# Twelve differences by adding transfers, bfloat16 operands read out of float32 tiles, and a new order of the last steps

## The chip, the core and the metric

The kernel runs on one core of one Trainium2 chip. TensorE (PE in the profile) multiplies matrices; VectorE (DVE) and ScalarE (ACT) work on elements; GpSimd (POOL) and SyncE (SP) here issue work to the 16 DMA engines ("queue" below is the list of transfers that an engine has issued). On-chip data lie in SBUF (128 partitions), results of matmuls in PSUM. The metric is the time of one execution on the device in microseconds; the time before is the median of three runs, 493.36 us (489.19 to 493.4).

## What is computed

Two independent results stand side by side in the output: a Fourier mixing of one input, and a long convolution of the other with kernels made of 128 decaying exponentials for each of 512 channels.

```python
# x: 2048 x 512; dft_seq: 2048 x 2048; dft_hid: 512 x 512
a = einsum("bsd,ed->bse", x, dft_hid_re)
b = einsum("bsd,ed->bse", x, dft_hid_im)
y1 = einsum("ts,bse->bte", dft_seq_re, a) - einsum("ts,bse->bte", dft_seq_im, b)
# u: 2048 x 512; A, C: 512 x 128 (complex); dt: 512
P = exp((A * dt[:, None])[:, :, None] * arange(2048))
K = 2 * einsum("dn,dnl->dl", C, P).real
y2 = irfft(rfft(u.T, 4096) * rfft(K, 4096), 4096)[:, :2048].T + u * D_skip
return concatenate([y1, y2], axis=-1)
```

## The kernel before

The host only rearranges and pads arrays and makes the constant matrices of the short Fourier transforms. One program then does both results at once, and its instructions are ordered by a planner written into the kernel (class `Plan`): each piece of work is a generator that yields the engine it wants and an estimate of its cost, and of all pieces that could start, the one with the earliest start, then the smallest "urgency", is issued next. The order on every queue is therefore fixed when the program is built. `act`, `dve` and `load` give the planner's estimates; `Sem` and `Ring` are counted buffers and `Event` a one-time signal of the planner.

**The Fourier part (`Fnet`).** The matrix along the sequence is loaded as given. Its rows are taken in groups of four that a Fourier matrix would make equal up to sign: for each of four column blocks t, for the sines (c = 1) and cosines (c = 0), and for k = 0 to 3, one load brings a `base` of 128 x 512 float32 and three more blocks of rows into a slot `raw` of 128 x 1536 float32 (`load_quad`, line 392; 32 such groups of rows in all, the `quads`). VectorE forms D, that is `rest` = `raw` plus or minus `base`, in bfloat16 (line 414, and line 419 where single rows have their own sign, k = 0). ScalarE rounds `base` to bfloat16 (`rough`, line 444) and sums the squares of D into a statistic (line 447), from which `guard` decides at the end whether D was small enough; if not, a plain program (`general`) does the Fourier part anew. On TensorE (`sums`, line 497) `base` is multiplied in float32 with the folded input (line 519), D in bfloat16 with the input's differences (line 522) and `rough` in bfloat16 with small parts of the input (`lows`, line 553; `middle`, line 548). `keep` and `keep_low` bring the sums to SBUF, `outputs` multiplies them with the other matrix (lines 611, 612). A base is free again after its four or five matmuls, `rest` too (two buffers), `rough` after its group of sums (six buffers).

**The convolution part (`Ssm`).** The kernels K come from tables of powers. The 512 channels are worked through in 16 chunks of 32. For each chunk ScalarE and VectorE make the seeds (`seed_args`, line 954: arguments by repeated doubling, reduced to half a turn in lines 970 and 972, clamped in line 974, then exponential and sine), and VectorE builds two tables by multiplications and additions (`tables1` and `tables2`, lines 923, 932, 946, 952, 1079). TensorE multiplies the two tables into the taps of the kernel (`taps`, line 1120). For each pair of chunks, 64 channels, `stage1_k` (line 1151) does the first step of the Fourier transform of K, and the result goes through memory (`xk`) to be reloaded in another order. The same is done to u (`stage1_u`, `xu`). The channels form five units of 128, 128, 128, 64 and 64. For each unit and quarter, `product` does the second step (line 1325), the complex product (lines 1355 and 1357; 1343 for the last unit) and the first step back (line 1371); the result `z` goes through memory (`zs`) and is reloaded transposed, and `inverse` does the last step (line 1442) and stores. For the last unit, 4, both trips through memory are replaced by transposes on VectorE (lines 1159 and 1422). The end of the kernel is therefore a chain: the last chunk's tables, its taps, the last `stage1_k` with its transposes, unit 4's product, its transposes, its last step, the store.

The order around the change is set by these lines:

```python
UNITS, LATE, BIGS = ((0, 128), (128, 128), (256, 128), (384, 64), (448, 64)), (3,), 3
FNET, GUARD, XTS = (2.0, 2.0, 2.0, 2.0), 2, 2
ISSUE, LAST_K, LAST_I, LATE_Z = 0.42, 7, 4, 3
BASES, SLOTS, RESTS, STAGED, ROUNDS = 3, 2, 2, 2, 6
GROUP_US, QUAD_US, AHEAD_US = 49.5, 9.0, 20.0
```

`FNET` is the urgency of the Fourier part's matmuls. A group's load isn't issued before GROUP_US x (its number // 4) + QUAD_US x (its number % 4) - AHEAD_US on the planner's clock. `LATE` names the unit whose product on VectorE waits until all tables are done.

Of the kernel before, what the change touches and what calls it, by code (L numbers as in the profile page):

```python
# [57 lines left out]
ARGS = 0.3  # L58
# [134 lines left out]
def load(kb):  # L193
    return max(0.55, kb / 330)


class Fnet:
# [11 lines left out]
    def __init__(self, tc, ctx, plan, x, wT, sT, out):  # L209
# [6 lines left out]
        self.ys, self.rounds = Sem(STAGED), Sem(ROUNDS)  # L216
# [153 lines left out]
    def loads(self, b):  # L370
# [3 lines left out]
        for n, i in enumerate(self.quads):  # L374
# [15 lines left out]
            self.plan.spawn(self.load_quad(i, slots), urgency)  # L390

    def load_quad(self, i, raw):
# [3 lines left out]
        first = i == self.quads[0]  # L396
# [13 lines left out]
        yield self.rests  # L410
        rest = self.pool.tile([128, 3, DM], BF16, name="rest", bufs=RESTS)

        def same(lo, hi, step, n, op):
            return v.tensor_tensor(rest[:, lo:hi:step], raw[:, lo:hi:step],  # L414
                                   base[:, None, :].to_broadcast([128, n, DM]), op=op)

        def own(lo, hi, sign):
            n = hi - lo
            return v.scalar_tensor_tensor(rest[:, lo:hi].rearrange("p n t -> p (n t)") if n == 1 else rest[:, lo:hi],
                                          base if n == 1 else base[:, None, :].to_broadcast([128, n, DM]),  # L420
                                          self.sign[:, sign:sign + 1],
                                          raw[:, lo:hi].rearrange("p n t -> p (n t)") if n == 1 else raw[:, lo:hi],
                                          op0=OP.mult, op1=OP.add)
        steps = {
            (0, 0): [(1536, lambda: same(0, 3, 1, 3, OP.subtract))],
            (0, 1): [(512, lambda: same(0, 1, 1, 1, OP.subtract)), (1024, lambda: same(1, 3, 1, 2, OP.add))],
            (1, 0): [(1024, lambda: same(0, 2, 1, 2, OP.add)), (512, lambda: same(2, 3, 1, 1, OP.subtract))],
            (1, 1): [(1024, lambda: same(0, 3, 2, 2, OP.add)), (512, lambda: same(1, 2, 1, 1, OP.subtract))],
        }[t // 2, c]
        if not k and (t, c) == (1, 0):  # L430
# [1119 lines left out]
```

## Time and profile before

| what | value |
|---|---|
| median of three runs | 493.36 us (489.19, 493.4, 493.36) |
| the profiled execution | 494.64 us |
| its span in the profile | 492.8 us |
| granted TensorE clock in it, mean | 0.932 of full speed |
| moved by the transfers | 110.42 MB, 224 GB/s over the span |

The span runs from the first to the last recorded instruction; the rest of the execution's time lies around it. In the profile a group of instructions is given as line, engine, operation, output<-inputs, shapes and count, then the busy time in us and the mean of one in ns, then the idle time of the engine just before them with what ended it. A float32 matmul shows as two records, its two passes. Matmuls are pipelined, so that their records overlap and a busy TensorE is not one at its peak; VectorE's records overlap a little too.

### The profile page before, as it was taken

How to read it: one execution, taken by the hardware profiler on the slowest of the kernel's cores; microseconds unless marked ns; L12 is line 12 of the kernel's file. 1: busy time of each engine (PE TensorE's matmuls, PEld its weight loads, DVE VectorE, ACT ScalarE, POOL GpSimd, SP SyncE). 2: the span in 40 equal slices, each digit the busy share in tenths (PEclk: the TensorE clock that was granted, in tenths of full speed). 3: DMA queues.
4: the chain of work that ended last, by engine and by line, in shares of the span. 5: the costliest groups of instructions: out<-in, count | busy, mean ns of one | idle time of the engine just before them, and what ended most of it. 6: DMA issues, size and time to landing. Idle time of an engine off the chain costs nothing. (4 is left out here: it accounts for less than half of the span.)

```text
span 492.8 us, 13631 instructions
## 1 busy us (share of the span) xinstructions
PE 396.8 (81%) x5630; PEld 200.9 (41%) x5674; DVE 440.8 (89%) x774; ACT 362.6 (74%) x725; POOL 0.9 (0%) x14
## 2 busy tenths in 40 slices
PE   3659977999869659989689877999997589788853
PEld 3213314344424425435253424454455254445642
DVE  3999997999999999999999999899999999996342
ACT  1658999999999697867597997879888896351420
POOL 0000000000000000000000000000000000000000
PEclk9977988999979897999899989999999799899995
DMA  8996794986558993878964299177678937965642
GB/s 292 359 352 200 275 354 171 306 289 238 156 194 261 283 281 98 274 196 283 343 202 165 50 285 319 46 209 244 205 247 228 253 94 224 227 179 211 177 132 63
DMA packets 130546, 110.42 MB, mean 224 GB/s; under 512 B 57136, under 2 KB 101552, under 8 KB 129968
## 3 DMA queue, kind: packets, MB, share of 16 engines
q1 hardware_dynamic: 122512, 106.48, 69.5%
q10 hardware_dynamic: 7968, 3.02, 2.2%
q8 instruction: 46, 0.75, 0.6%
q14 instruction: 20, 0.16, 0.1%
HBM read 77.04 MB, written 32.44 MB: 222 GB/s over the span
## 5 line engine op out<-in xcount | busy, mean ns | idle before, releaser
L923 DVE TENSOR_TENSOR prod<-t,cs 128x1024 f32<-128x1024 f32 (+4 forms) x160 | 125.1, 798 | 5.0 <-ACT t L1038 3.5
L611 PE MATMUL f<-p,w 128*128 128x512 f32 x128 | 70.2, 630 | 7.8 <-ACT y L636 5.7
L932 DVE TENSOR_TENSOR t<-prod 128x512 f32<-128x512 f32 (+4 forms) x160 | 73.6, 477 | 0.6
L447 ACT ACTIVATE slots<-rest 128x1536 f32<-128x1536 bf16 x32 | 47.4, 1481 | 14.6 <-DVE rest L414 13.5
L414 DVE TENSOR_TENSOR rest<-slots,base 128x512 bf16<-128x512 f32 (+2 forms) x52 | 53.6, 1034 | 0.7 <-PE f L522 0.5
L519 PE MATMUL f<-base,es 128*128 128x512 f32 x64 | 39.8, 708 | 13.7 <-ACT bes L332 6.6
L1120 PE MATMUL f<-t,t 128*32 128x80 f32 x2048 | 42.0, 238 | 10.7 <-DVE t L932 5.7
L1120 PEld LDWEIGHTS f<-t,t 128*32 128x32 f32 x2048 | 37.6, 112 | 20.3 <-issue 10.3
L939 ACT ACTIVATE square<-t 128x256 f32<-128x256 f32 (+1 forms) x64 | 36.6, 571 | 12.1 <-DVE t L932 6.8
L1079 DVE TENSOR_TENSOR t<-t,cs 128x1024 f32<-128x1024 f32 x32 | 39.0, 1220 | 0.0
L519 PE MATMUL f<-base,ec 128*128 128x512 f32 x64 | 36.5, 653 | 0.0
L611 PEld LDWEIGHTS f<-p,w 128*128 128x128 f32 x128 | 22.3, 193 | 32.0 <-issue 16.8
L522 PE MATMUL f<-rest,xi 128*128 128x512 bf16 x88 | 28.4, 422 | 7.9 <-DVE rest L414 5.5
L522 PE MATMUL f<-rest,xr 128*128 128x512 bf16 x88 | 26.3, 397 | 7.5 <-DVE rest L414 6.0
L1325 PE MATMUL f<-big,w 64*32 64x256 f32 (+1 forms) x960 | 27.4, 358 | 4.7 <-issue 3.3
L1350 ACT ACTIVATE big<-f 128x1024 f32<-128x1024 f32 x26 | 25.8, 1026 | 4.3 <-PE f L1325 4.3
L952 DVE TENSOR_TENSOR t<-square 128x128 f32<-128x128 f32 (+1 forms) x64 | 24.8, 387 | 1.2 <-ACT square L939 1.1
L522 PEld LDWEIGHTS <-xi 128*128 128x128 bf16 x96 | 9.8, 104 | 36.6 <-issue 28.2
L798 ACT ACTIVATE mid<-f 128x512 f32<-128x512 f32 x24 | 13.2, 591 | 14.0 <-PE f L1371 14.0
L1325 PEld LDWEIGHTS f<-big,w 64*32 64x32 f32 x960 | 16.0, 108 | 17.3 <-issue 8.4
L946 DVE SCALAR_TENSOR_TENSOR t<-t 128x128 f32<-128x128 f32 (+2 forms) x48 | 22.4, 466 | 0.4
L522 PEld LDWEIGHTS <-xr 128*128 128x128 bf16 x96 | 9.7, 101 | 31.6 <-issue 28.1
(174 smaller groups left out, 720.7 us busy)
## 6 DMA issues: line engine op xcount, KB each, us to landing
slots<-in_sT SPq DMA_DIRECT2D x31, 768.0 KB, 5.6
xu<-big SPq DMA_DIRECT2D x16, 512.0 KB, 4.1
base<-in_sT SPq DMA_DIRECT2D x31, 256.0 KB, 4.8
big<-xu SPq DMA_DIRECT2D x13, 512.0 KB, 7.3
big<-xk SPq DMA_DIRECT2D x13, 512.0 KB, 6.9
xk<-big SPq DMA_DIRECT2D x6, 1024.0 KB, 7.0
zs<-mid SPq DMA_DIRECT2D x11, 512.0 KB, 4.5
big<-zs SPq DMA_DIRECT2D x10, 512.0 KB, 7.9
```

Of the source, the lines that this page charges most:

```text
L414: return v.tensor_tensor(rest[:, lo:hi:step], raw[:, lo:hi:step], base[:, None, :].to_broadcast([128, n, DM]), op=op)
L447: nc.scalar.activation(raw, rest, AF.Square, accum_out=self.stat[:, n:n + 1])
L519: nc.tensor.matmul(out, x[:, cols], base, start=k == 0, stop=False)
L522: nc.tensor.matmul(out, still[:, cols], rest[:, h], start=False, stop=k == 3 and h == 2)
L611: nc.tensor.matmul(ps, self.w[k][:, cols], self.p[t, c][:, d], start=k == 0, stop=False)
L923: self.nc.vector.tensor_tensor(p.rearrange("p k d c m -> p k (d c) m"), src.rearrange("p d c l -> p (d c) l")[:, None, :, rows].to_broadca ...
L932: self.nc.vector.tensor_tensor(dst[:, :, :, rows], p[:, 0], p[:, 1, :, ::-1], op=OP.add)
L939: self.nc.scalar.activation(sq, t[:, :, :, m // 2:m], AF.Square)
L1079: self.nc.vector.tensor_tensor(t[:, :, ::1 - 2 * k, 48 + 16 * k:64 + 16 * k], t[:, :, :, 1:32:2], cs[:, k, 5, :, :, None].to_broadcast([12 ...
L1120: nc.tensor.matmul(ps[32 * j:32 * j + 32, i], t1[:, d, c], t2[:, d, c], start=c == 0, stop=c == 1, tile_position=(0, 32 * j))
L1325: nc.tensor.matmul(both[:, :, c], self.w2[rows, R * q + r, xx, 32 * c:32 * c + 32], xs[rows, r, xx], start=True, stop=True, tile_position= ...
L1350: a.activation(flat[:, 1024 * m:1024 * m + 1024], p.rearrange("p b d -> p (b d)"), AF.Copy)
```

## The change

- **D.** For twelve groups of rows (`ADDED`: the sines of each t, k = 1, 2, 3) D is no longer made by VectorE. `base` is loaded once more into those blocks of `raw` to which it is to be added (one transfer with a repeated source), ScalarE writes -`base` into the block from which it is to be subtracted, and a transfer issued by GpSimd adds the rows from memory onto `raw`. For the other twenty groups VectorE makes D in place, in float32.
- **Upper halves.** There is no `rest` and no `rough` tile. The bfloat16 matmuls read the upper two bytes of each float32 of D and of `base` (`[:, :, 1]` of the tile seen as bfloat16), which truncates where the copies rounded. The squares are taken from the float32 D, by a piece of its own (`squares`) that starts after the group's matmuls; a slot is held until then, a base until the end of its group of sums. Six bases and three slots in place of three and two.
- **Arguments.** The reduction and clamp of the phase are done once on the parameters (`params`), before the doubling, and the clamp of each chunk goes.
- **The end.** Unit 3's results are turned by VectorE like unit 4's (`TURNED`). The last chunk's table, taps and the last K stage run in halves: the first half of the taps starts when half the table is there, and `last_stage1_k` does the last 64 channels in two steps, one for each chunk.
- Urgencies and due times are new.

```diff
-ARGS = 0.3
+ARGS = 1
...
-        self.bases, self.rests, self.acc_left = Sem(BASES), Sem(RESTS), {}
+        self.bases, self.acc_left = Sem(BASES), {}
...
         base = self.pool.tile([128, DM], F32, name="base", bufs=BASES)
-        first = i == self.quads[0]
+        plus, minus = {(0, 0): (None, slice(0, 3)), (0, 1): (slice(1, 3), slice(0, 1)), (1, 0): (slice(0, 2), slice(2, 3)),
+                       (1, 1): (slice(0, 3, 2), slice(1, 2))}[t // 2, c]
+        own, first = not k and ((t, c) == (1, 0) or t >= 2), i == self.quads[0]
+        if i in ADDED:
+            yield from self.added(i, base, raw, plus, minus)
+        else:
+            yield from self.subtracted(i, base, raw, plus, minus, first, own)
+        rough = base.bitcast(BF16).rearrange("p (t e) -> p t e", e=2)[:, :, 1]
+        rest = raw.rearrange("p h t -> p (h t)").bitcast(BF16).rearrange("p (h t e) -> p h t e", h=3, e=2)[:, :, :, 1]
+        self.m[i] = base, rest, rough, raw
+        self.plan.set(self.m_ev[i])
+    def added(self, i, base, raw, plus, minus):
+        nc, (t, c, k) = self.nc, i
+        n = len(range(3)[plus]) if plus else 0
+        yield "dma", load(256 * (1 + n))
+        nc.sync.dma_start(base, self.sT[t, c, k, 0])
+        if n:
+            nc.sync.dma_start(raw[:, plus], self.sT[t, c, k, 0][:, None, :].to_broadcast([128, n, DM]))
+        m = len(range(3)[minus])
+        yield "act", act(512 * m)
+        nc.scalar.activation(raw[:, minus], base[:, None, :].to_broadcast([128, m, DM]), AF.Copy, scale=-1.0)
+        yield "dma", 1.6 * load(768)
+        nc.gpsimd.dma_start(raw, self.sT[t, c, k, 1:].rearrange("h p t -> p h t"), accum_op=OP.add)
+        yield "landed" + str(i), 1.0
+    def subtracted(self, i, base, raw, plus, minus, first, own):
+        nc, v, (t, c, k) = self.nc, self.nc.vector, i
...
-        yield self.rests
-        rest = self.pool.tile([128, 3, DM], BF16, name="rest", bufs=RESTS)
-        def same(lo, hi, step, n, op):
-            return v.tensor_tensor(rest[:, lo:hi:step], raw[:, lo:hi:step],
-                                   base[:, None, :].to_broadcast([128, n, DM]), op=op)
...
+        def same(at, op):
+            n = len(range(3)[at])
+            return 512 * n, lambda: v.tensor_tensor(raw[:, at], raw[:, at], base[:, None, :].to_broadcast([128, n, DM]),
+                                                    op=op)
...
+        if not own:
+            steps = [same(at, op) for at, op in ((plus, OP.add), (minus, OP.subtract)) if at]
...
         for n, step in steps:
             yield "dve", dve(n)
             step()
-        yield self.rounds
-        rough = self.pool.tile([128, DM], BF16, name="rough", bufs=ROUNDS)
-        self.m[i] = base, rest, rough
-        self.plan.set(self.m_ev[i])
-        yield "act", act(512)
-        nc.scalar.activation(rough, base, AF.Copy)
+    def squares(self, i, base, raw):
+        (t, c, k), a = i, self.nc.scalar
         n = 8 * t + 4 * c + k
         yield "act", act(1536) + 0.1
-        nc.scalar.activation(raw, rest, AF.Square, accum_out=self.stat[:, n:n + 1])
+        a.activation(raw, raw, AF.Square, accum_out=self.stat[:, n:n + 1])
         if not k:
             yield "act", act(512) + 0.1
-            nc.scalar.activation(raw[:, 0], base, AF.Square, accum_out=self.stat[:, 38 + n // 4:39 + n // 4])
+            a.activation(raw[:, 0], base, AF.Square, accum_out=self.stat[:, 38 + n // 4:39 + n // 4])
...
-            self.plan.put(self.bases)
-            self.plan.put(self.rests)
+            self.plan.spawn(self.squares((t, c, k), base, raw), SQUARES)
...
-            self.plan.put(self.rounds)
+            self.plan.put(self.bases)
...
+        yield "dve", dve(n, 2)
+        v.tensor_scalar(k, par[:, 1], RND, RND, op0=OP.add, op1=OP.subtract)
+        yield "dve", dve(n)
+        v.tensor_tensor(par[:, 1], par[:, 1], k, op=OP.subtract)
+        yield "dve", dve(n, 2)
+        v.tensor_scalar(par[:, 1], par[:, 1], 0.5, -0.5, op0=OP.min, op1=OP.max)
...
-        yield "dve", dve(n, 2)
-        v.tensor_scalar(r, r, 0.5, -0.5, op0=OP.min, op1=OP.max)
...
-            yield from self.halves("prod", t, slice(0, 16), cs[:, :, 10], slice(16, 32))
+            self.t1[n] = t
+            yield from self.halves("prod", t, slice(0, 16), cs[:, :, 10], slice(16, 32), n == 15 and self.t1_half)
...
+            evs = [Event() for _ in range(2)]
             for m in range(2):
-                self.plan.spawn(self.taps(ks, 2 * n + m, one), 0.5)
-            self.plan.spawn(self.stage1_k(ks, n, ev), 0.5)
+                self.plan.spawn(self.taps(ks, 2 * n + m, one, evs[m]), 0.5)
+                if n == LAST_K:
+                    self.plan.spawn(self.last_stage1_k(ks, m, evs[m]), 0.5)
+            if n < LAST_K:
+                self.plan.spawn(self.stage1_k(ks, n, ev), 0.5)
...
+            if last:
+                if o:
+                    yield self.t1_ev[n]
+                yield "pe", 1.25, None, 129
...
+            if last and not o:
+                self.plan.spawn(self.first_taps(ks, p), 0)
...
+    def first_taps(self, ks, p):
+        yield "act", act(320)
+        self.nc.scalar.activation(ks[:, 8:12].rearrange("p i l -> p (i l)"), p[:, 0, :320], AF.Copy)
+        self.plan.set(self.half_taps)
+    def last_stage1_k(self, ks, m, ev):
+        nc, n = self.nc, LAST_K
+        yield self.const_ev
+        yield self.last_xt
+        yield self.t1_half if m else ev
+        got = yield from self.banks(2)
+        yield ev
+        yield "pe", 1.5, None, 41
+        i = slice(8 * m, 8 * m + 8)
+        for a, j in ((a, j) for a in range(4) for j in range(4)):
+            r = slice(32 * j, 32 * j + 32)
+            out = got[j // 2][1].rearrange("p h t -> p (h t)")[:, 256 * (j % 2 + 1):256 * (j % 2 + 2)]
+            out = out.rearrange("p (i e m) -> p i e m", i=8, e=2)
+            taps = (ks[r, i, :32].rearrange("p i (m e) -> p i e m", e=2),
+                    ks[r, i, 32:64].rearrange("p i (e m) -> p i e m", e=2), ks[r, i, 64:],
+                    self.dskip[r, 16 * n + 8 * m:16 * n + 8 * m + 8])[a]
+            to = (out, out, out[:, :, 1], out[:, :, 0, 0])[a]
+            nc.tensor.matmul(to, self.f1k_last[r, a % 3 > 0], taps, start=a == 0, stop=a == 3, tile_position=(32 * j, 0))
+        if m:
+            self.plan.put(self.kss)
+        for h, (k, p) in enumerate(got):
+            yield "dve", dve(512, 0.6)
+            to = self.xt4.rearrange("p (x n j i d) -> p n j i d x", n=2, j=4, i=2, d=8)[:, 1, 2 * h:2 * h + 2, m]
+            nc.vector.transpose(to, p.rearrange("p h t -> p (h t)")[:, 256:768].rearrange("p (i e m) -> p i m e", i=16, e=2))
+            self.give(k)
+        self.k_left -= 1
+        if not self.k_left:
+            self.plan.set(self.last_k)
...
-            if i >= LAST_I and not q:
-                self.zt = yield from self.big.take()
+            if i in TURNED and not q:
+                self.zt[i] = yield from self.big.take()
...
-        last = i >= LAST_I
+        last = i in TURNED
         if last:
             self.give_tile(self.mid, qflat)
-            z = self.zt.rearrange("p (q r x d) -> p q r x d", q=2, r=R, x=4)[:, q]
+            z = self.zt[i].rearrange("p (q r x d) -> p q r x d", q=2, r=R, x=4)[:, q]
...
-UNITS, LATE, BIGS = ((0, 128), (128, 128), (256, 128), (384, 64), (448, 64)), (3,), 3
-FIRST_TABLE, T1, SEEDS = 0.01, 0.005, 1.5
+UNITS, LATE, TURNED, BIGS = ((0, 128), (128, 128), (256, 128), (384, 64), (448, 64)), (3,), (3, 4), 3
+FIRST_TABLE, T1, SEEDS = 0.01, 0.005, 0.5
 UNIT = 0.05
-FNET, GUARD, XTS = (2.0, 2.0, 2.0, 2.0), 2, 2
+ADDED = [(t, 1, k) for t in range(4) for k in (1, 2, 3)]
+FNET, GUARD, XTS = (1.5, 1.5, 1.5, 1.5), 2, 2
 ISSUE, LAST_K, LAST_I, LATE_Z = 0.42, 7, 4, 3
-BASES, SLOTS, RESTS, STAGED, ROUNDS = 3, 2, 2, 2, 6
-GROUP_US, QUAD_US, AHEAD_US = 49.5, 9.0, 20.0
+BASES, SLOTS, STAGED, SQUARES = 6, 3, 2, 1.5
+GROUP_US, QUAD_US, AHEAD_US = 46, 11, 25
```

More of the change, by code (lines that the diff above doesn't have):

```diff
@@ L1028, in halves @@
             yield from self.add(p, t[:, d], to)
+            if ev and not d.start:
+                self.plan.set(ev)
     def tables1(self):
@@ L1143, in stage1_k @@
+        got = yield from self.banks(2)
         yield "pe", 2.7, None, 57
@@ L1172, in stage1_k @@
         yield done
-        if last:
-            self.plan.set(self.last_k)
-            return
         unit = max(n // 2, n - 3)
```

109 lines of the change are left out of this document (50 added, 59 removed).

## The prediction

> **What bounds the kernel now.** I read the page first, then the busy times by stage, the waits of VectorE, and the timeline of the end.
>
> ```profile
> span 492.8 us, 13631 instructions
> ## 1 busy us (share of the span) xinstructions
> PE 396.8 (81%) x5630; PEld 200.9 (41%) x5674; DVE 440.8 (89%) x774; ACT 362.6 (74%) x725; POOL 0.9 (0%) x14
> ```
> ```profile
> 20.00:442.00 422.00, 352.76 (x4728) 171.26 (x4770) 408.35 (x729) 343.99 (x687) 0.00 (x0) 0.94 0.74 228
> 442.00:492.80 50.80, 32.98 (x874) 23.71 (x874) 21.06 (x29) 11.62 (x20) 0.00 (x0) 0.88 0.51 151
> ```
> ```profile
> 30.00:80.00 50.00, 40.73 (x119) 12.99 (x121) 48.34 (x89) 42.63 (x91) 0.00 (x0) 0.84 0.80 272
> 80.00:130.00 50.00, 48.14 (x409) 20.69 (x410) 46.80 (x87) 48.20 (x97) 0.00 (x0) 0.99 0.69 238
> 130.00:180.00 50.00, 38.99 (x617) 19.58 (x623) 49.07 (x86) 43.19 (x86) 0.00 (x0) 0.90 0.86 255
> ...
> 280.00:330.00 50.00, 40.11 (x668) 20.86 (x668) 46.74 (x86) 41.63 (x82) 0.00 (x0) 0.97 0.73 205
> 330.00:380.00 50.00, 45.51 (x590) 23.16 (x592) 48.95 (x85) 42.27 (x82) 0.00 (x0) 1.00 0.78 242
> ```
> ```profile
> DVE prod L923 <- ACT t L1038: 3.5, 2, 2.8
> ```
>
> The rows that begin with A:B give, for that stretch, the busy time of PE, PEld, DVE, ACT and POOL, then the granted clock, the DMA share and GB/s. From 20 to 442 us VectorE is busy 408.35 of 422 us, 97%, and its longest total wait there is 3.5 us: this stage ends when VectorE's list of work ends. TensorE (352.76, 84%) and ScalarE (343.99, 82%) have room, the transfers (0.74) too. POOL has nothing there. In the last 50.8 us VectorE is busy for 21.06 only: a different limit, a chain.
>
> ```profile
> 441.65 0.69 DVE L932 TENSOR_TENSOR t<-prod 128x512 f32<-128x512 f32 x1
> ...
> 444.87 2.28 PE L1120 MATMUL f<-t,t 128*32 128x80 f32 x120
> ...
> 449.77 2.48 PE L1151 MATMUL f<-ks,t 32*128 32x512 f32 x24
> ...
> 452.42 3.72 DVE L1159 STREAM_TRANSPOSE t<-f 128x512 f32<-128x512 f32 x4 [4.48 <-PE f L1151]
> ...
> 461.89 2.03 PE L1325 MATMUL f<-t,w 64*32 64x128 f32 x128
> ...
> 478.35 4.35 DVE L1422 STREAM_TRANSPOSE t<-t 128x512 f32<-128x512 f32 x4
> ...
> 488.32 0.39 SPq L786 DMA_DIRECT2D out_yb<-t  x1
> ```
>
> Columns: start, duration, engine, line. The last operation on a decay table ends at 442.34; then taps (L1120), their copy, the last K stage (L1151), its transposes, which end at 456.14, the last unit's product (L1325) at 461.89, the transposes of its result, the last store at 488.32. So the time is 442.3 us set by VectorE's work, and 50.5 us set by that chain.
>
> **The change, part by part.**
>
> ```profile
> L932 DVE TENSOR_TENSOR t<-prod 128x512 f32<-128x512 f32 x64 | 44.0, 687 | 0.3
> ...
> L414 DVE TENSOR_TENSOR rest<-slots,base 128x1024 bf16<-128x1024 f32 x20 | 24.4, 1220 | 0.7 <-PE f L522 0.5 <-DMA slots<-in_sT 0.2
> ...
> L414 DVE TENSOR_TENSOR rest<-slots,base 128x512 bf16<-128x512 f32 x25 | 17.1, 685 | 0.0
> ...
> L974 DVE TENSOR_SCALAR seed<-seed 128x352 f32<-128x352 f32 x16 | 5.4, 338 | 0.0
> ```
> ```profile
> 116.24 0.69 DVE L414 TENSOR_TENSOR rest<-slots,base 128x512 bf16<-128x512 f32 x1
> 116.84 1.22 DVE L923 TENSOR_TENSOR prod<-t,cs 128x1024 f32<-128x1024 f32 x1
> ```
>
> *D without VectorE.* Each of the twelve groups (sine rows, k = 1 to 3 of each of four t) had one subtraction or addition of 1024 columns (1220 ns) and one of 512 (685 ns). In the timeline the next instruction starts 0.60 us after a 512 one of 0.69 (116.24 to 116.84), so a record costs its length less 0.09. Removed: 12 x (1.13 + 0.595) = 20.7 us. The other twenty groups keep their operations; the output grows from bfloat16 to float32, and the float32 additions of 512 columns in L932 (687 ns against 685) say that this is free.
>
> *Arguments.* The clamp (L974) goes: 16 x (0.338 - 0.09) = 4.0 us. In its place three operations run twice, on 480 columns and on 32: on 480 each lies between L974's 0.25 and the 0.595 of 512 columns, so 0.75 to 1.8 us together, and the short ones are at most half of that; I take 1.5 in all. VectorE's list becomes 408.35 - 20.7 - 4.0 + 1.5 = 385.2 us.
>
> What the stage then takes depends on how full VectorE stays. At the present 0.968 it is 398 us, a gain of 24; at the fill of the poorest stretch quoted (46.74 of 50, 0.935) 412, a gain of 10. TensorE must fit 352.76 in it and so goes from 84% to 87% or more, and the adding transfers make arrivals later. I take the middle: 405 us, **a gain of 17 us**, the tables ending at 425.
>
> *ScalarE.*
>
> ```profile
> L444 ACT ACTIVATE rough<-base 128x512 bf16<-128x512 f32 x32 | 19.9, 622 | 0.0
> ```
>
> The rounded copy of each base goes (32 x 0.622 = 19.9 us). Twelve negations of 512 columns come (12 x 0.62 = 7.5). The squares keep their length, but move behind the matmuls. Net 12 us less on an engine with slack: nothing in the sum; what covers it is that VectorE is fuller.
>
> *The transfers.* Nothing like an adding transfer from POOL's queue is in the trace.
>
> ```profile
> slots<-in_sT SPq DMA_DIRECT2D x31, 768.0 KB, 5.6
> ...
> base<-in_sT SPq DMA_DIRECT2D x31, 256.0 KB, 4.8
> ```
>
> These are KB and median us from issue to landing. Now a group is on its way for 5.6 us and is then worked on by VectorE for 1.9 (1.22 + 0.69): 7.5. Then: base lands (4.8), ScalarE negates (0.62), the adding transfer lands. Bounds for that transfer: 5.6 us, as the plain load of 768 KB, or 11.2, if the old contents have to be fetched as a second stream; it can't be below 5.6, since the same rows come from memory. So 11 to 16.6 us. I take 13, nearer to the plain load, and nothing in the sum, because the plan now asks for groups 25 us ahead, not 20, and has three slots, not two. If that cover is gone it is the first rival. The base also comes two more times for each of the twelve groups: 24 x 256 KB, 6.3 MB beside 110.4. SP's queue keeps two issues for such a group, and the third is POOL's. POOL's queue is empty, so nobody waits behind its wait for ScalarE's negation; on ScalarE itself the negation waits for the base, and the table squares queued behind would wait with it, if the plan has the landing wrong.
>
> [...]
>
> *Upper halves.* bfloat16 matmuls now read every second bfloat16 of float32 tiles. The trace has no such read.
>
> ```profile
> 121.38 0.81 PE L522 MATMUL f<-rest,xi 128*128 128x512 bf16 x3
> 122.03 1.02 PE L519 MATMUL f<-base,es 128*128 128x512 f32 x2
> 122.89 0.81 PE L522 MATMUL f<-rest,xi 128*128 128x512 bf16 x3
> ```
> ```profile
> L1243 PE MATMUL f<-big,ib 64*128 64x512 f32 x64 | 19.1, 678 | 0.0
> ...
> L1151 PE MATMUL f<-ks,f1k 32*128 32x512 f32 x112 | 14.3, 625 | 0.9 <-ACT ks L1125 0.8
> ```
>
> Three bfloat16 matmuls start 0.65 us before the next work (121.38 to 122.03), 0.217 each; two float32 passes take 0.86, 0.43 each. Bounds: 0 (a dense read can't be the slower one), or the pace of float32, 0.215 more. I take 0: half of L1151's float32 matmuls of 512 columns read every second element, and the whole group's mean is 625 ns, against 678 where all reads are dense (L1243). The skip costs nothing there. It is a float32 read, though, so the other end stays as a rival.
>
> [...]
>
> *The end.* Of the last chunk's taps and of the last K stage the first half now runs before the tables end. After it remain: half the taps (2.28 us for 120 of 128 records, so 1.2), a copy of 320 columns (0.4, by L444's 0.62 for 512), half of L1151 (2.48, so 1.3), two of four transposes (1.9), and four hand-overs of some 0.25 (0.17 from L1151 at 452.25 to the transposes), 1.0: 5.8 us, where it took 13.8 (442.34 to 456.14). The 5.75 us from there to L1325 were TensorE's work for units 2 and 3, which must still be done, before or beside. Unit 3's results stay on the core: its bounce through memory goes, which was not on the chain, and VectorE gets four more transposes (4.4 us by L1422) and two copies of 0.7 in a stretch where it has 29.7 us free. Bounds: the start of L1325 comes 8 to 13.8 us earlier relative to the tables' end; the displaced TensorE work (5.75) and unit 3's work (5.8) delay the rest by 0 to 11.5. So -3.5 to +13.8; I take **a gain of 6**, a little above the middle (5), because the two engines have half of this stretch free.
>
> *Priorities and due times* (sums, seeds, arguments; bases held to the end of their group of sums, six of them): they reorder VectorE's list and do not shorten it; 0, with what they hurt in the first rival.
>
> Sum, against the profiled execution (494.64 us, 1.84 more than its span): 494.64 - 17 - 6 = 471.6. That execution is 1.28 above the median of 493.36, so **470**. The ends are 494.6 - 24 - 13.8 - 1.3 = 455 and 494.6 - 10 + 3.5 - 1.3 = 487.
>
> **Rivals.** *First: the adding transfers come late and TensorE waits in VectorE's place.* Each of twelve groups arrives 3.5 to 9 us later than now, 42 to 109 in all, and with four of six bases held until a group of sums ends, the next group's third load can't start before. For it: no row for such a transfer. Against it: TensorE has 50 us of other work to put in (405 - 353). If the waits eat the gain of VectorE and only the end's gain is left: 494.6 - 6 - 1.3 = 487, from 478 to 500.
>
> *Second, on the other side: the skipping reads run at float32's pace.* Records per run: 192 of L522, 64 of L553, 48 of L548: 304 x 0.215 = 65 us more on TensorE, 418 in the stage. It decides from where TensorE is over some 0.94 of 405 us, so from 28 us, 0.09 us for each read. TensorE at 0.963 (48.14 of 50, the fullest stretch quoted) needs 434 us, at 0.91 (45.51) 459: against 422 now, with the end's gain, 494.6 + 12 - 6 - 1.3 = 499 to 524; 511. For it: float32 passes are slower in just this ratio. Against it: L1151.
>
> *Third: the transfers become the bound.* 0.74 x 422 = 312 us of them now, plus 24 x 256 KB and 12 x 768 KB read twice, 15.7 MB, at the 272 GB/s of the stretch from 30 us, whose share is 0.80: 58 us x 0.80 = 46. That is 358 of 405, 0.88, and no quoted stretch has more than 0.86 (from 130 us). At 0.80 the stage needs 448 us: 494.6 + 26 - 6 - 1.3 = 513. Against it: the second reads are only an upper bound, and without them the share is 330 of 405, 0.82.
>
> **How the numbers follow.** My forecast 0.60 (455 to 487), the late transfers 0.22, the slow reads 0.11, the transfers as bound 0.07. Faster by over 1% (below 488.4; about what the spread of the three times, 489.2 to 493.4, lets one tell): all of the first and some half of the second, 0.72. Within 1%: 0.09, from the second. Slower: 0.11 + 0.07 and the second's rim, 0.19. The range 455 to 500 leaves out the two slow cases, 0.18. The predicted time is the likeliest case's.
>
> **What would show it.** Right: VectorE busy for some 423 us in all (440.8 - 23.2 + 5.8); the last table operation near 425; from it to the last K stage's transposes 6 to 8 us; ScalarE near 350; bfloat16 matmuls still 0.217 apart. Wrong: pitch of 0.43 (second rival); waits of TensorE on a transfer or of ScalarE on a base, and VectorE below 93% ahead of the tables' end (first); a DMA share near 0.9 with plain loads landing in 8 us (third). A tail that is as long as before would mean that the engines, not the chain, set it.

## The result, and the profile after

The changed kernel takes 508.09 us (median of four runs, 505.56 to 510.35), the kernel before 493.38 in the same comparison (489.19 to 493.83): a ratio of 1.029, with a 95% interval of 1.024 to 1.034. It is slower, where 470 was forecast. Executions over 1.5% above the fastest of the same kernel count in the medians of this document, not in its ratios. The profiled execution took 510.35 us, with a span of 508.5.

The page's first part for the changed kernel:

```profile
span 508.5 us, 13662 instructions
## 1 busy us (share of the span) xinstructions
PE 396.9 (78%) x5660; PEld 204.3 (40%) x5706; DVE 425.5 (84%) x746; ACT 351.6 (69%) x704; POOL 16.4 (3%) x26
```

VectorE lost what it was to lose (425.5 us busy, forecast 423), and so did ScalarE (351.6, forecast 350). The work went; the time did not. Busy time by stage, up to the end of the last table operation and from there on (busy PE, PEld, DVE, ACT, POOL, then clock, DMA share and GB/s):

```profile
20.00:443.43 423.43, 337.29 (x4585) 167.27 (x4624) 388.70 (x690) 325.26 (x654) 14.18 (x11) 0.91 0.85 241
443.43:508.50 65.07, 49.12 (x1049) 31.16 (x1053) 25.30 (x40) 19.87 (x33) 0.00 (x0) 0.94 0.31 100
```

The tables end at 443.4, as before (442.3), though VectorE now needs 388.7 us for the stage in place of 408.4: it stands idle for 34.7 of 423.4 us, where it stood idle for 13.7. The DMA share is 0.85 in place of 0.74. And what follows the tables' end is 65 us long in place of 51, with 49.1 us of TensorE's work in it in place of 33.0.

TensorE's waits (engine, tile and line, what ended them; us in total, times, longest):

```profile
PE f L543 <- DMA slots<-in_sT: 37.4, 5, 13.3
PE f L543 <- DVE slots L442: 9.9, 4, 4.7
```

The first row is new. L543 multiplies D, and it waits for the transfer that adds. Some rows of the timeline show the longest of these waits being made:

```profile
20.35 0.67 SPq L414 DMA_DIRECT2D base<-in_sT  x1
...
37.77 1.48 ACT L468 ACTIVATE slots<-slots 128x1536 f32<-128x1536 f32 x1 [7.91 <-PE f L543]
...
39.65 0.61 ACT L419 ACTIVATE slots<-base 128x512 f32<-128x512 f32 x1
...
40.69 1.28 POOL L421 DMA_DIRECT2D slots<-in_sT  x1 [16.23 <-ACT seed L993]
...
41.87 0.34 DVE L997 TENSOR_SCALAR seed<-seed 128x352 f32<-128x352 f32 x1 [2.49 <-ACT seed L995]
...
53.96 1.01 PE L543 MATMUL f<-slots,xi 128*128 128x512 bf16 x2 [13.35 <-DMA slots<-in_sT]
```

L468 takes the squares of a group. They now stand behind the matmuls on that group, so ScalarE waited 7.91 us for TensorE; the negation for the next group (L419), whose base had been issued at 20.35, stood behind them in ScalarE's queue; POOL's adding transfer was issued at 40.69; TensorE stood still until 53.96. TensorE was late because a transfer was late, which made ScalarE late, and through it the next transfer. VectorE, which has nothing to do with these D any more, is held up the same way: its next seed operation (L997) waited for ScalarE, whose work on the seeds stood behind the same squares. The largest of VectorE's waits in the stage, and the one of ScalarE for the squares:

```profile
DVE seed L997 <- ACT seed L995: 5.9, 5, 2.5
DVE y L321 <- DMA out_ya<-y: 4.7, 1, 4.7
DVE slots L442 <- DMA slots<-in_sT: 4.5, 4, 2.0
```
```profile
ACT slots L468 <- PE f L543: 13.7, 5, 7.9
```

The end of the timeline:

```profile
442.74 0.69 DVE L959 TENSOR_TENSOR t<-prod 128x512 f32<-128x512 f32 x1
...
449.86 1.96 DVE L1205 STREAM_TRANSPOSE t<-f 128x512 f32<-128x512 f32 x2 [2.10 <-PE f L1199]
450.08 1.06 PE L573 MATMUL f<-base,bec 128*128 128x512 bf16 x3 [0.26 <-ACT p L597]
...
494.07 0.38 SPq L807 DMA_DIRECT2D out_yb<-t  x1
...
502.82 0.35 ACTq L652 DMA_DIRECT2D out_ya<-y  x1
```

The last K stage's transposes (L1205) end at 451.82, 8.4 us after the tables, where it took 13.8 and 5.8 was forecast: that part of the new end did its work. But the last sums (L573) run at 450.08. In the timeline of the kernel before, the same sums were L553:

```profile
392.61 1.06 PE L553 MATMUL f<-rough,bec 128*128 128x512 bf16 x2 [0.22 <-issue]
```

The Fourier part is 57 us later, its outputs (L652) leave the chip at 502.82, and they, not the last unit's store (494.07), now end the run.

### The profile page after: what moved, and what is told of

Its sections match the earlier page's. It is cut to its first block, busy times and chain, and to the rows that moved or that the text cites. A ratio compares the mean times of both kernels' runs of the same rounds, so it can differ in the third digit from the quotient of the medians.

```text
span 508.5 us, 13662 instructions
## 1 busy us (share of the span) xinstructions
PE 396.9 (78%) x5660; PEld 204.3 (40%) x5706; DVE 425.5 (84%) x746; ACT 351.6 (69%) x704; POOL 16.4 (3%) x26
## 3 DMA queue, kind: packets, MB, share of 16 engines
q0 software_dynamic: 4800, 9.44, 11.3%
## 5 line engine op out<-in xcount | busy, mean ns | idle before, releaser
L631 PE MATMUL f<-p,w 128*128 128x512 f32 x128 | 68.9, 620 | 6.7 <-ACT y L656 5.8
L468 ACT ACTIVATE slots<-slots 128x1536 f32<-128x1536 f32 x32 | 47.3, 1479 | 19.1 <-PE f L543 13.7
L543 PE MATMUL f<-slots,xi 128*128 128x512 bf16 x86 | 30.1, 449 | 38.2 <-DMA slots<-in_sT 37.4
L1157 PE MATMUL f<-t,t 128*32 128x80 f32 x2048 | 44.5, 247 | 6.6 <-issue 3.1
L1157 PEld LDWEIGHTS f<-t,t 128*32 128x32 f32 x2048 | 40.5, 118 | 16.4 <-issue 8.8
L543 PEld LDWEIGHTS <-xi 128*128 128x128 bf16 x96 | 10.1, 106 | 66.4 <-issue 49.8
L442 DVE TENSOR_TENSOR slots<-slots,base 128x512 f32<-128x512 f32 (+2 forms) x28 | 31.0, 1107 | 4.5 <-DMA slots<-in_sT 4.5
L631 PEld LDWEIGHTS f<-p,w 128*128 128x128 f32 x128 | 22.5, 191 | 30.4 <-issue 17.2
L543 PE MATMUL f<-slots,xr 128*128 128x512 bf16 x86 | 26.5, 403 | 10.1 <-DVE slots L442 9.6
L819 ACT ACTIVATE big<-f 128x512 f32<-128x512 f32 x40 | 22.7, 597 | 16.3 <-PE f L1227 6.9
L421 POOL DMA_DIRECT2D slots<-in_sT x12 | 15.6, 1299 | 380.3 <-DVE slots L442 107.9
L979 DVE TENSOR_TENSOR t<-square 128x128 f32<-128x128 f32 (+1 forms) x64 | 24.9, 389 | 3.4 <-ACT square L966 3.2
L1439 PE MATMUL f<-big,ia 32*64 32x256 f32 x448 | 18.8, 421 | 9.1 <-DVE big L1425 5.0
L1393 PEld LDWEIGHTS f<-big,w 64*32 64x32 f32 x1024 | 18.8, 111 | 16.5 <-issue 9.4
```

What stands on the lines that cost most here:

```text
L442: return 512 * n, lambda: v.tensor_tensor(raw[:, at], raw[:, at], base[:, None, :].to_broadcast([128, n, DM]), op=op)
L468: a.activation(raw, raw, AF.Square, accum_out=self.stat[:, n:n + 1])
L543: nc.tensor.matmul(out, still[:, cols], rest[:, h], start=False, stop=k == 3 and h == 2)
L631: nc.tensor.matmul(ps, self.w[k][:, cols], self.p[t, c][:, d], start=k == 0, stop=False)
L1157: nc.tensor.matmul(ps[32 * j:32 * j + 32, i], t1[:, d, c], t2[:, d, c], start=c == 0, stop=c == 1, tile_position=(0, 32 * j))
L1393: nc.tensor.matmul(both[:, :, c], self.w2[rows, R * q + r, xx, 32 * c:32 * c + 32], xs[rows, r, xx], start=True, stop=True, tile_position= ...
```

## The experiments

Each ratio is to the kernel before, run beside it on the same chip, with its 95% interval. In the two kernels that leave D unfinished in twelve groups (e5, e6) and in e17, the squares come out large, so the plain program runs behind the planned one; their totals of 1056 to 1071 us contain both, and only what lies before it is read.

### Adding transfers, urgencies, the end: what costs?

e1, no adding transfers:

```
-ADDED = [(t, 1, k) for t in range(4) for k in (1, 2, 3)]
+ADDED = []
```

> The changed kernel with no adding transfers: the twelve groups get their D by VectorE's subtraction and addition again; bases held, three slots, new urgencies, new arguments and new end stay. Theory A (the adding transfers come late: TensorE waits for them, the sums of all four t shift, and the Fourier results become the end): 495 us or less, TensorE's waits on the D groups nearly gone (37 us after, under 15 here), last sums before 415 instead of 443. Rival B (urgencies and held bases alone make the sums late): still 503 to 513, last sums still near 440. Rival C (the new end with unit 3's transposes does it): still near 508, with the last sums early and the end long.

Measured: 491.44 us, ratio 0.995 (0.993 to 0.998). No row of TensorE's waits names a D group's transfer, and the last sums run at 385.9. Theory A.

e2, the urgencies and due times of before, with adding transfers:

> The changed kernel with the five urgency and due-time lines as before (arguments 0.3, seeds 1.5, sums 2.0, due times 49.5, 9 and 20); adding transfers, held bases and new end stay. Theory A: it stays slow, 500 us or more, since the transfers are what comes late. Rival B: back to 493 or below.

Measured: 521.81, ratio 1.054 (1.050 to 1.058). TensorE waits 35.8 us for the D groups' transfers. The urgencies are not the cause; with the adding transfers in place the kernel is better off with the new ones (1.029).

e3, both undone:

> Both undone: no adding transfers and the urgencies of before; left of the change are the reads of upper halves with bases held to the end of a group of sums, three slots, the new arguments and the new end. Theory A: 485 to 495, the last sums at 385 to 400, as before. If held bases and slots alone make the sums late: 500 or more, last sums beyond 410.

Measured: 498.91, ratio 1.008 (1.005 to 1.011), the last sums at 397.8. Without adding transfers the Fourier part is early under either set of urgencies; the total missed the expected range by 4 us.

e4, the kernel before with the new end and the new arguments alone (the class `Fnet` and the constants of before, the rest of the changed kernel):

> The kernel before, its Fourier part and its urgencies untouched, with the new end (half tap copies, half K stage, unit 3 transposed on the core) and the new arguments alone. By the terms of the prediction: 4.0 - 1.5 us of VectorE and 6 of the end, so about 485 (480 to 490). Rival C (the new end costs): 493 or more, with unit 4's chain no earlier than before.

Measured: 503.85, ratio 1.023 (1.016 to 1.029). A miss: two parts that were to gain 8.5 us lost 10, and no adding transfer is in this kernel. The tables end at 454.9, with VectorE's list 411.0 us long. That needed runs of its own, below.

### Is it the adding, or what stands around it?

e5, no adding (`ADDED` is empty, as in e1) and no VectorE operation either, for the twelve groups:

```
-        for n, step in steps:
+        for n, step in [] if c and k else steps:
             yield "dve", dve(n)
```

> The changed kernel without adding transfers, in which the twelve groups get plain loads of the base and of the 768 KB, and neither VectorE nor a transfer forms their D: 24 VectorE operations are left out, and the sums multiply the loaded rows as they are. It shows what 20.7 us of VectorE's list are worth if nothing is paid for them. If VectorE's list sets the tables' end, as the prediction had it: 491.4 - 17 = 474 (470 to 479). If another bound stands close behind (TensorE, or the hand-overs between VectorE and ScalarE): 482 to 490.

Busy time to the tables' end of e1, and then of e5:

```profile
20.00:449.45 429.45, 368.91 (x4871) 179.68 (x4875) 409.50 (x723) 330.28 (x663) 0.00 (x0) 0.93 0.72 225
```
```profile
20.00:431.55 411.55, 355.08 (x4613) 168.96 (x4611) 389.50 (x695) 324.69 (x655) 0.00 (x0) 0.95 0.73 231
```

VectorE's list is 20.0 us shorter and the tables end 17.9 us earlier, which is the prediction's 17. But the last unit's last store is issued at 481.8, against 486.3 in e1: only 4.5 of the 17.9 us reach the end (in one execution of each). In between unit 3's product waits for its data from memory, and the last unit stands behind it:

```profile
446.25 3.67 PE L1393 MATMUL f<-slots,w 64*32 64x128 f32 x128 [4.68 <-DMA slots<-xk]
...
458.31 1.79 PE L1393 MATMUL f<-t,w 64*32 64x128 f32 x111
```

The second row is the last unit's product, 26.8 us after the tables' end; in e1 it starts at 461.8, 12.3 us after it.

e6, the transfers from POOL write and do not add; every engine has the same instructions in the same order as in the changed kernel:

```
-        nc.gpsimd.dma_start(raw, self.sT[t, c, k, 1:].rearrange("h p t -> p h t"), accum_op=OP.add)
+        nc.gpsimd.dma_start(raw, self.sT[t, c, k, 1:].rearrange("h p t -> p h t"))
```

> The changed kernel with the twelve transfers from POOL not adding but writing: the 768 KB, the queue, the wait for ScalarE's negation and the order on every engine are the same, the addition is left out. Theory A1 (the adding itself is slow: old contents fetched as well): landing near 6.6 us in place of 9.3, 495 to 502. Theory A2 (base, negation and load in series, with POOL's issue of 1.29 us, is what is late): 505 to 511, landing still over 8.5.

The part of the page on transfers, for the stretch from 0 to 430 us: queue, packets, MB, share of the sixteen engines' time; then issues, count, KB, median us to landing. The changed kernel, and then e6:

```profile
q0 software_dynamic: 4800, 9.44, 13.3%
...
slots<-in_sT SPq DMA_DIRECT2D x19, 768.0 KB, 6.6
slots<-in_sT POOLq DMA_DIRECT2D x12, 768.0 KB, 9.3
...
base<-in_sT SPq DMA_DIRECT2D x31, 256.0 KB, 5.5
...
slots<-in_sT SPq DMA_DIRECT2D x12, 512.0 KB, 6.4
```
```profile
q0 software_dynamic: 2496, 9.44, 6.4%
...
slots<-in_sT SPq DMA_DIRECT2D x19, 768.0 KB, 5.8
slots<-in_sT POOLq DMA_DIRECT2D x12, 768.0 KB, 6.9
```

The same 9.44 MB take 13.3% of 430 us when they are added, 57.2 us of all sixteen engines, and 6.4%, 27.5 us, when they are written: 2.1 times, in 1.9 times the packets. An adding transfer lands 2.4 us later, and the plain loads beside it 0.8. What it does to the run, in e6:

```profile
20.00:429.69 409.69, 337.53 (x4625) 166.93 (x4624) 387.50 (x689) 323.85 (x654) 8.39 (x11) 0.93 0.80 248
```
```profile
46.90 1.44 PE L543 MATMUL f<-slots,xi 128*128 128x512 bf16 x3 [10.28 <-DMA slots<-in_sT]
...
436.33 1.06 PE L573 MATMUL f<-base,bec 128*128 128x512 bf16 x4 [0.26 <-ACT p L597]
...
479.24 0.38 SPq L807 DMA_DIRECT2D out_yb<-t  x1
...
487.99 0.35 ACTq L652 DMA_DIRECT2D out_ya<-y  x1
```

The tables end at 429.7, 13.7 us earlier, and the last output leaves at 488.0, 14.8 us earlier. Since the order is the same, the lag can be read along it: the matmul that ran at 53.96 runs at 46.90 here, 7.1 us earlier; by the tables' end the lag is 13.7. Half of it arises in the first group of sums, most of the rest by 220 us (the same matmul of the outputs, L631, at 219.67 against 208.58). One execution of each is compared, and the profiled one of the changed kernel is its slowest (510.35, where the fastest took 505.56). The expected figure of 495 to 502 stands in the total, which can't be read; an estimate from the last output is 510.35 - 14.8, some 495.5. The landing of 6.9 is theory A1's. A2 has its share as well: TensorE still waits 25.2 us for these transfers, since base, negation and transfer still follow one another, and the last sums are still at 436.3, so the Fourier outputs still come last. In e5, which has no such series, the tables end at 431.6, hardly later, but the last sums run at 395.5. By the estimate, the new way would at best be about as fast as e1 (491.44) even if the adding cost nothing.

e17, e6 with a second copy that nobody waits for (the lines that set aside its place in memory, `spare_dram`, are left out here):

```
-        nc.gpsimd.dma_start(raw, self.sT[t, c, k, 1:].rearrange("h p t -> p h t"))
+        for to in (raw, self.spare_dram[3 * t + k - 1]): nc.gpsimd.dma_start(to, self.sT[t, c, k, 1:].rearrange("h p t -> p h t"))
```

> As the run in which the twelve transfers from POOL write and do not add, but behind each of them POOL issues a second transfer of the same 768 KB to a place in memory that nobody reads or waits for; the order on the engines is the same. It brings back the load that the adding put on the transfers (57.2 against 27.5 us of all sixteen, before 430 us) without its later landing. Only what lies before the general path is compared: the tables ended at 443.4 with adding and at 429.7 with writing. If the load on the transfers is what cost the 13.7 us: 440 to 445. If the later landing of the group itself did: 429 to 433. In between, both.

```profile
q0 software_dynamic: 4992, 18.88, 12.3%
...
slots<-in_sT SPq DMA_DIRECT2D x19, 768.0 KB, 6.6
slots<-in_sT POOLq DMA_DIRECT2D x12, 768.0 KB, 7.6
```
```profile
20.00:435.05 415.05, 342.00 (x4625) 167.26 (x4624) 388.13 (x689) 324.35 (x653) 16.68 (x22) 0.92 0.85 267
```

The load on the transfers is back (52.9 us; a DMA share of 0.85, plain loads at 6.6 us, both as in the changed kernel), and the tables end at 435.05: 5.4 of the 13.7 us. That leaves 8.3 for the later landing of the groups themselves (9.3 against 7.6), by subtraction. One execution of each stands behind this split, and runs of one kernel differ by up to 5 us (505.56 to 510.35), so it says that both matter, not in which ratio.

e7, nine adding transfers, none in the first t:

```
-ADDED = [(t, 1, k) for t in range(4) for k in (1, 2, 3)]
+ADDED = [(t, 1, k) for t in range(1, 4) for k in (1, 2, 3)]
```

> Adding transfers for nine groups, not for the three of the first t, whose three waits of TensorE took 24.0 us in the changed kernel. Theory: the start is the greater part of the loss; without it 495 to 500 and no wait of TensorE for a D group before 80 us. If the loss is spread over all four t: 503 to 508.

Measured: 509.05, ratio 1.037 (1.029 to 1.045). Both expected ranges are missed, the second by 1 us. The waits before 80 us are gone, as expected, and nothing is won: TensorE waits for these transfers for 16.7 us in all, in place of 37.4, 13.90 of them in one wait that ended at 147 us, but the tables end at 444.3 and the last sums are at 450.1. So the loss is not the sum of TensorE's waits. The start is where the loss showed first, not where it has to arise.

e8, a later hand-over in the plan's price:

```
-        yield "landed" + str(i), 1.0
+        yield "landed" + str(i), 5.0
```

> The changed kernel with its hand-over after an adding transfer priced 4 us longer in the plan (5.0 in place of 1.0), so that the order of work on each engine counts on a later arrival; work, transfers and urgencies are the same. If the order was planned for arrivals that are too early, and that makes most of the loss: 495 to 500. If the late arrival itself is the loss, whatever the order: 504 to 512.

Measured: 502.71, ratio 1.023 (1.016 to 1.030), between the two. TensorE's waits for these transfers fall from 37.4 to 24.9 us and the last sums come at 416.3, so that the outputs are out before the last unit is; the tables end at 449.7. A longer price, or the other order that it makes, mends some of the loss: a third by the medians, a fifth by the ratios, whose intervals overlap. The transfers still land in 10.0 us.

### What an order is worth by itself

The loss of e4 had no adding transfer behind it. Three kernels took it apart: e9, the kernel before with the new arguments alone; e10, with the new end alone; and e11, a control with nothing changed but a due time:

```
-GROUP_US, QUAD_US, AHEAD_US = 49.5, 9.0, 20.0
+GROUP_US, QUAD_US, AHEAD_US = 49.75, 9.0, 20.0
```

> The kernel before with the new arguments alone (rounding and clamp on the parameters, no clamp in the seeds). By the terms of the prediction VectorE loses 4.0 - 1.5 = 2.5 us: 491 (489 to 494). Rival D (the arguments cost what the new end with them lost): 500 or more, with the first seeds later than before. Rival E (any edit reshuffles the planned order, and the order by itself moves the time by 5 to 10 us): anything from 488 to 503, with no wait that names the arguments.

> The kernel before with the new end alone (no new arguments): with the run before it, it splits the 503.85 us of both together. By the terms of the prediction: 494 - 6 = 488. Rival C (the new end costs): 500 or more. Rival E: anything from 486 to 503, the stretch from the tables' end to the last unit's store shorter than the 46 us of before, and the tables' end late for no wait that names the end.

> A control: the kernel before with one due time of its load groups at 49.75 in place of 49.5, so that the order of work changes and nothing else. If an order's luck is small: 491 to 496. Rival E: off by 5 us or more, to either side.

Measured: the arguments 506.53, ratio 1.024 (1.018 to 1.030); the end 488.32, ratio 0.990 (0.984 to 0.996); the control 503.01, ratio 1.017 (1.011 to 1.023). The new end did what the prediction's terms say; the arguments came out as rival D had it, with the first seeds 3.2 us later (35.3 against 32.2); and the control is rival E's case: a due time moved by a quarter of a microsecond, with the same work, costs 8.4 us. VectorE in the control, and then in e10, to the tables' end:

```profile
20.00:449.50 429.50, 361.80 (x4629) 174.99 (x4631) 408.68 (x729) 341.64 (x685) 0.00 (x0) 0.92 0.71 222
```
```profile
20.00:444.30 424.30, 360.04 (x4866) 173.73 (x4866) 410.28 (x732) 344.29 (x689) 0.00 (x0) 0.93 0.74 229
```

The control's list is that of before (408.68 us), and the engine idles 20.8 us over it in place of 13.7, in many short waits for ScalarE (the longest row is 5.9 us in six). Nothing in it is broken; it is another order. The granted clock doesn't explain it: at 0.931 the control took 500.28 us and the kernel before 493.1. Nor does it explain the main result: the kernel before took 495.23 at 0.917, the changed kernel 510.35 at 0.919.

e12 was a try for a version below both:

> No adding transfers, and the due times of groups at 49.5 in place of 46 with the sums at urgency 1.0 in place of 1.5; the rest as in the changed kernel. A try for a version below both: 484 to 489 if held bases, new arguments and new end are each worth something; 490 to 494 if the order decides.

Measured: 492.89, ratio 0.999 (0.996 to 1.002). That is where it was to be if the order decides; it shows no more than that the parts don't add up.

Four more pairs asked whether the arguments cost something in every order, as rival D would have it. e13 is the changed kernel with the arguments of before, e14 and e15 are e1 and e3 with them, e16 is the control with the new arguments:

> The changed kernel with the arguments of before (clamp in the seeds, none on the parameters); adding transfers and all else stay. If the new arguments cost some 12 us in any order: 494 to 499. If what they cost alone was the luck of one order: 500 to 515, since the adding transfers are still there.

> No adding transfers and the arguments of before; new urgencies, held bases and new end stay. Pair of the run without adding transfers (491.44). If the arguments cost 12 us in any order: 477 to 482. If it was one order's luck: 486 to 500.

> No adding transfers, urgencies and arguments of before; left are the held bases with reads of upper halves, three slots and the new end. Pair of the run at 498.91. If the arguments cost 12 us in any order: 485 to 489. If one order's luck: 489 to 503.

> The new arguments alone on the control with the due time at 49.75 (503.01). If they cost 12 us in any order: 512 to 518. If one order's luck: 494 to 508.

All four came out in the range for one order's luck. Ratios to the kernel before, without and with the new arguments:

| order | old arguments | new arguments | difference |
|---|---|---|---|
| kernel before | 1 | 1.024 (e9) | +2.4% |
| with the new end | 0.990 (e10) | 1.023 (e4) | +3.3% |
| changed kernel | 1.042 (e13) | 1.029 | -1.3% |
| without adding transfers | 1.009 (e14) | 0.995 (e1) | -1.4% |
| the same, old urgencies | 1.015 (e15) | 1.008 (e3) | -0.7% |
| control | 1.017 (e11) | 1.005 (e16) | -1.2% |

Four are negative and two positive, with a mean of +0.2%: the arguments have no cost of their own that these runs can tell. What e9 and e4 lost is best read as the luck of an order, since the control lost 1.7% without any new work.

The table answers the main question once more. Adding against not adding, by the line of `ADDED` alone (the planner then lays out the order anew), is 1.029 against 0.995, 1.054 against 1.008 (e2, e3), and 1.042 against 1.009 (e13, e14): 3.3 to 4.6% in each of three orders, and TensorE waits 37.4, 35.8 and 36.8 us for the D groups' transfers in the three that add, and not at all in the three that don't.

e18, the new end alone on the control:

> The new end alone on the control with the due time at 49.75 (503.01). If the end's gain holds in another order: 495 to 499, and from the tables' end to the last unit's last store 37 to 43 us in place of 47.3. If it was one order's luck: 500 to 508, with 45 us or more there.

Measured: 501.81, ratio 1.013 (1.005 to 1.021), against 1.017 for the control. In this order the end is worth 1 us, within the intervals nothing; from the tables' end to the last store its slowest execution took 47.0 us, where 37 to 43 was expected if the gain held.

## Why the prediction was wrong

**The step that failed** is the one on the transfers: "I take 13, nearer to the plain load, and nothing in the sum, because the plan now asks for groups 25 us ahead, not 20, and has three slots, not two." Both halves fell. By the medians the three terms are 5.5 us for the base, 0.6 for the negation and 9.3 for the transfer (POOL's issue is in it): 15.4, not 13. But from the issue of its base to the landing of its adding transfer a group took 15.8 to 33.6 us, 20 in the middle. The sum had left out that the second copy of the base (512 KB, 6.4 us to landing) must land as well, and that each step stands in a queue behind other work: the third group's negation ran 19.3 us after its base was issued. And the cover was not there: the next slot comes free after the squares, the squares wait for TensorE, and TensorE was waiting, so a late group made the next one late. In the first group of sums the loads of the next slots (L430) were issued at 28.60 and 39.37, just as the squares that began at 27.00 and 37.77 ended. Set against e6, the adding alone is worth 13.7 us at the tables' end, and the whole way of making D in the transfers, set against e1, 16.7 us of the time (508.09 against 491.44). The forecast had 17 to the good, so this step makes some 34 of the 38 us between 470 and 508.

**VectorE's part was right, and didn't pay.** Where D cost nothing, a list 20.0 us shorter ended 17.9 us earlier (e5); the forecast was 17. With the adding transfers all of it turned into idle time (34.7 us in the stage, 22.2 in e6). But even D for nothing brought only 4.5 us to the last store: unit 3's trip through memory and the last unit's work behind it were next in line. The forecast carried the 17 us through to the end as if nothing else stood there.

**The rivals.** The first named the right mechanism, and its signs came: TensorE waits on the transfers, and VectorE is 92% busy ahead of the tables' end. But it gave 487, 500 at most, because it let the end's gain stand. It missed that TensorE's waits push back the Fourier part as a whole, whose last sums came at 450.1 in place of 392.6, so that its outputs took over the end. The third had the load nearly exact: it reckoned 358 us of transfers if the old contents are read a second time, and the stage shows 0.85 of 423.4, 360. Its price of 513 us came closer than the forecast's, but by luck: its signs, a share near 0.9 and plain loads landing in 8 us, did not come (0.85 and 6.6). The two were weighed as separate cases (0.22 and 0.07), though one cause, a transfer that takes the engines 2.1 times as long (57.2 us in place of 27.5), feeds both: it lands late and delays the others. The second rival fell. In the changed kernel:

```profile
124.65 0.84 PE L543 MATMUL f<-slots,xi 128*128 128x512 bf16 x3
125.33 1.02 PE L540 MATMUL f<-base,es 128*128 128x512 f32 x2
```

Three reads of every second bfloat16 start 0.68 us before the next work, 0.227 each, where dense ones took 0.217: 304 of them make 3 us on TensorE, where 0 was taken and 65 feared.

**The end** had the right size in one order: the new end alone took 6.3 us off the median of before (494.6 to 488.3 in their comparison), and 6 was forecast. In two other orders it was worth 2.7 us (e4 against e9) and 1.2 (e18 against e11). Two of the last stage's transposes now lie ahead of the tables' end and lengthen VectorE's list there (410.28 in e10 against 408.35 us), which the forecast had put at nothing.

**Priorities and due times** were put at 0, and the arguments at 2.5 us to the good. The arguments changed VectorE's list by anything from 0.6 us more to 2.6 less. Beside that stands the order: with the work unchanged, another one cost 8.4 us in the control. The forecast's range had no term for that.

POOL's twelve issues took 1.28 to 1.41 us each in the changed kernel and 0.76 to 0.87 in e6. Their length did not follow VectorE's work: in the changed kernel the third, during which VectorE was busy for 0.10 us, took 1.28, and the nine after it, during each of which VectorE was busy for 1.12 us or more, took 1.28 or 1.29. In e6, from the same queue and in the same order, the transfer without its addition landed 2.4 us earlier: that part of the lateness lay in the adding. Why the same bytes take 57.2 us of all sixteen engines when they are added and 27.5 when they are written, no run shows.

What stays open: in which ratio load and late landing make the 13.7 us, which short waits make one order 8 us worse than another, and how much of what e6 leaves over belongs to the series of base, negation and transfer and how much to the order.

## What to carry to other kernels

Work that is moved off a full engine into the transfers is not free: price an adding transfer as two transfers (here 57.2 us of all sixteen engines in place of 27.5), and follow who waits for it and what those waits hold back, for here the next slot was loaded only when the late group's squares were done. Before counting a shorter list as time won, ask what ends next; here 17.9 us of VectorE's time were worth 4.5. And where a planner lays out the order, run a control with a change that should mean nothing: here it moved the time by 8.4 us, so a single edit in a single order proves little, and pairs in several orders prove more. The best kernel seen is the one before with the new end alone, at 0.990 of its time (0.984 to 0.996), and even that gain did not hold in another order (e18).

## What was not expected of the hardware

The same 9.44 MB from POOL's queue went in 4800 packets when added and in 2496 when written, and POOL spent 1.29 us on each issue in place of 0.76. In e6 a plain transfer of 768 KB landed only 1.1 us later from POOL's queue (6.9) than from SP's (5.8).
